# Moving the keys' adding transfers behind GpSimd's second long product, and one matrix product into the start, in a fused attention and feed-forward kernel

## The chip, the cores and the metric

The kernel runs on one core of one Trainium2 chip. The metric is the device time of one execution in microseconds; the median of several runs is compared. TensorE does matrix products, VectorE (DVE), ScalarE (ACT) and GpSimd (POOL) the elementwise work, and SyncE (SP) and GpSimd issue transfers.

## The reference

Attention over keys that are averaged over 4 x 4 places, for 4 batches of 12,288 queries with 128 channels and 768 keys, then a feed-forward layer of width 2048 with g = h - tanh(h):

```
kv_pool = kv.reshape(B, H // r, r, W // r, r, C).mean(axis=(2, 4))   # r = 4
k = v = kv_pool.reshape(B, -1, C) @ w_sr
s = (q @ k.T) / sqrt(C);  a = exp(s - s.max(-1));  a /= a.sum(-1) + 1e-09
x = a @ v
h = x @ w_in;  out = (h - tanh(h)) @ w_out
```

## The kernel before

**Groups and steps.** The queries go in 96 groups of 512, 24 for each batch. A group is 8 steps (UN) of the schedule. `attention` computes scores, exponentials and shares of a group some 20 steps ahead, `feed_forward` the 16 blocks of the hidden layer, in pairs, so 8 per group. The hidden function is a cubic around a centre, so every batch has its own scaled weights (`winr`, `Wr`), slopes (`At`, `Ah`) and centre (`cen`), which `keys` and `about_centre` prepare while the batch before it runs.

**Order.** No engine chooses at run time. Every operation is given to `Plan.op` with a due step, an engine, an assumed duration and the tiles it reads and writes. `Plan.run` plays this through once, with those durations, and the order that comes out is the order in which each engine's instructions are written. A tile named in an operation's reads orders the plan; on the chip an instruction waits only for what it really touches. Operations with `lane=True` keep the order of their due steps on their engine. `bank(.., "x", ..)` names one PSUM bank that is used by many in turn.

**GpSimd in a steady group.** In this order: `dr` (L832, the rounded part of the attention result), `z` = v + 1 (L903), [an adding transfer of the next batch's keys, L366, when there is one], `z` = z * v (L907, the first long product), the first adding transfer of the shares (`rs`, L797), `rp` = z * v (L907, the second long product), `dl` (L858), `ql` (L812), the second adding transfer of the shares (L797). `rp` feeds the last matmuls of `acc` in TensorE (L927), whose end lets ScalarE write the result `o` (L938).

**Keys of batches 2 to 4.** The 16 places are summed by transfers into one tile, `kvp`: one plain transfer from SP and 15 adding ones from GpSimd's queue, one per group, from `GATHER` groups ahead of the batch. Each waits for the one before it. Behind the last, VectorE sums the rows (L428) and takes the mean (L432).

**Keys of batch 1.** Twelve pieces of 64 keys are loaded at the start (L380), each with 16 values per key. VectorE sums eight of them (L394), GpSimd folds pieces 2, 5, 8 and 11 in four steps (L388). Ten matmuls (five of 512 columns, `warm`, L414) run on the summed pieces and their result is not used. Then come the mean (L433), `centre` (L440) and the first products with the centre (L536). The loads of the output weights and of q are ordered behind the sum of piece 6 (`HELD`).

**Norm of the input weights.** 16 matmuls `winT` x `winT` (32 instructions, fp32 takes two each; L333), a copy (L337) and one more product (L346) are due at step 16, in the steady groups.

Of the kernel before, what the change touches and what calls it, by code (L numbers as in the profile page):

```python
# [22 lines left out]
KB = 64  # L23
WN = 512
# [132 lines left out]
def attention_then_ffn(ctx: ExitStack, tc: tile.TileContext, q, kv_by_key, kv_by_place, w_sr, w_in,  # L157
                       w_out, out):
    nc = tc.nc
    V, A, PL, PE, SP = nc.vector, nc.scalar, nc.gpsimd, nc.tensor, nc.sync  # L160

    B, C, N = q.shape
    K, W = kv_by_key.shape[1], kv_by_key.shape[2]
    F = w_in.shape[1]
    KT, FT = K // P, F // P
    KH, UN, AN = K // 2, FT // 2, KT // 2
    NG = N // G
# [6 lines left out]
    dram = ctx.enter_context(tc.tile_pool(name="dram", bufs=1, space=DRAM))  # L174
    plan = Plan(tc)

    DIRECT, HELD = 2, 6
    BUFS = {"kc": 2, "kvp": 1, "kTr": 2, "vvr": 2, "Mn": 1, "Mh": 2, "A": 2, "Ah": 2, "Wg": 3, "Wr": 2,
            "winr": 2, "q": 4, "qr": 5, "ql": 2, "E": 2, "r2": 7, "rs": 3, "t": 2, "dl": 1, "df": 1, "dr": 2, "u": 3, "r": 4,
            "rp": 2, "v": 2, "z": 1, "o": 2, "row": 2, "col": 2, "At": 2, "hb": 2, "W2": 1,  # L180
# [2 lines left out]
    def sb(key, tag, shape, dt=F32, step=-1e6):  # L183
        n = BUFS[tag]
        plan.tile(key, tag, n, lambda: wk.tile(shape, dt, tag=tag, name=tag, bufs=n), step)

    def big(key, step):
        plan.tile(key, "big", 3, lambda: ps.tile([P, WIDE], F32, tag="big", name="big", bufs=3), step)

    def bank(key, tag, step):  # L190
        plan.tile(key, tag, 1, lambda: ps.tile([P, G], F32, tag=tag, name=tag, bufs=1), step)
# [6 lines left out]
    winT = const.tile([P, FT, C], F32, name="winT")  # L198
# [3 lines left out]
    ident = const.tile([P, P], F32, name="ident")  # L202
# [102 lines left out]
    def weights(step, load_step):  # L305
        NW = F // WN
        for n in range(NW):
            words_of(step + n, load_step + n / 8, n, "i")
        for j in range(2):
            turned = f"turned.{j}"  # L310
            big(turned, step + NW + j)
            for k in range(2):
                def turn(j=j, k=k, turned=turned):
                    for f in range(8 * j + 4 * k, 8 * j + 4 * k + 4):
                        PE.matmul(out=plan[turned][:, (f % 8) * P : (f % 8 + 1) * P],
                                  lhsT=win32[:, f * P : (f + 1) * P], rhs=ident,
                                  start=True, stop=True)

                plan.op(step + NW + j, "PE", 1.0, turn, (("win32", 2 * j + k), "ident"),
                        ((turned, k),), late=0.2)  # L320

            def copy(j=j, turned=turned):
                A.copy(out=winT[:, 8 * j : 8 * j + 8].rearrange("p t c -> p (t c)"), in_=plan[turned])

            plan.op(step + NW + j, "ACT", 1.03, copy, (turned,), (("winT", j),), late=0.1)
        s = 16.0
        bank("WW", "x", s)
        sb("WW32", "W2", [P, P])
        bank("W4", "x", s + 1)

        def product():
            for f in range(FT):
                PE.matmul(out=plan["WW"][:, 0:P], lhsT=winT[:, f], rhs=winT[:, f], start=(f == 0),  # L333
                          stop=(f == FT - 1))

        def copy_product():
            A.copy(out=plan["WW32"], in_=plan["WW"][:, 0:P])  # L337

        plan.op(s, "PE", 4.0, product, ("winT",), ("WW",), late=0.2)
        plan.op(s, "ACT", 0.3, copy_product, ("WW",), ("WW32",), late=0.1)  # L340
        norm(s + 1, "WW32", "W4", B)

    def norm(step, of, at, n):

        def square():
            PE.matmul(out=plan[at][:, 0:P], lhsT=plan[of], rhs=plan[of], start=True, stop=True)  # L346

        def rows():
            V.tensor_reduce(out=norms[:, n : n + 1], in_=plan[at][:, 0:P], op=ALU.add, axis=AX.X,
                            apply_absolute_value=True)  # L350

        plan.op(step, "PE", 0.25, square, (of,), (at,), late=0.2)
        plan.op(step, "DVE", 0.3, rows, (at,), (("norms", n),))

    def keys(b, s0):

        kvp, row, cen, kTr, vv32, vvr, Mn = (
            f"{x}.{b}" for x in ("kvp", "row", "cen", "kTr", "vv32", "vvr", "Mn"))
# [3 lines left out]
        NK = K // KB  # L362
        for w in range(W if b else 0):
            def gather(w=w):
                if w:
                    PL.dma_start(out=plan[kvp], in_=kv_by_place[b - 1, w], accum_op=ALU.add)  # L366
                else:
                    SP.dma_start(out=plan[kvp], in_=kv_by_place[b - 1, w])

            at = (b * NG - GATHER[b - 1] + max(w - 1, 0)) * UN + AT["more"][0] - 2 * UN  # L370
            plan.op(at - (0.01 if w else 4), *(("POOL", 0.87) if w else ("SP", 0.5)), gather, (), (kvp,),
                    late=3.0, dma=1.0, lane=w > 0)
        for j in range(0 if b else NK):
            gap = 0.1
            s, key = s0 - gap * (NK - j) - 2, f"kc.{b}.{j}"
            sb(key, ("E", "r", "rp", "kc", "r", "r")[j % 6], [P, KB, W])
            at = slice(j * KB, (j + 1) * KB)

            def load(at=at, key=key):
                SP.dma_start(out=plan[key], in_=kv_by_key[:, at, :])  # L380

            plan.op(s - 8, "SP", 0.5, load, (), (key,), late=2.0, dma=1.27)
            if j % 3 == 2:
                for k, w in enumerate((8, 4, 2, 1)):
                    def fold(key=key, w=w, at=at):
                        x = plan[key]
                        to = plan[kvp][:, at].unsqueeze(2) if w == 1 else x[:, :, 0:w]
                        PL.tensor_tensor(out=to, in0=x[:, :, 0:w], in1=x[:, :, w : 2 * w], op=ALU.add)  # L388

                    plan.op(s + k / 8, "POOL", 0.2 + KB * w * 0.0021, fold, (key,),  # L390
                            ((kvp, j),) if w == 1 else (key,))
            else:
                def pool(key=key, at=at):
                    V.tensor_reduce(out=plan[kvp][:, at], in_=plan[key], op=ALU.add, axis=AX.X)  # L394

                plan.op(s, "DVE", 1.2, pool, (key,), ((kvp, j), "held") if j == HELD else ((kvp, j),))
# [5 lines left out]
        sb(Mn, "Mn", [P, C])  # L402
        Mh = f"Mh.{b}"
        sb(Mh, "Mh", [P, 2, C], R32)
        apart_by = (1, 5.3, 8, 8)[b]
        s1, s2, s3, s4 = (s0 + n * apart_by for n in range(1, 5))
        s4 = s4 if b else 24.0
        for x, at in ((pc, s0), (pm, s3), (p4, s4)):
            bank(x, "x", at)
        if b == 0:  # L410
            big("warm", s0 - 3)
            for j in range(WN // KB - 1, NK):
                def warm(j=j):
                    PE.matmul(out=plan["warm"][:, 0:WN], lhsT=ident,  # L414
                              rhs=plan[kvp][:, (j + 1) * KB - WN : (j + 1) * KB], start=True,
                              stop=True)

                plan.op(s0 - 3, "PE", 1.2, warm, ["ident"] + [(kvp, i) for i in range(j + 1)],
                        ("warm",))
        big(pk, s1)  # L420
        big(pv, s2)

# [71 lines left out]
        for j in range(2):  # L494
            plan.op(s2 + j / 4, "PE", 0.7, partial(product_by_key, j), ("wsr", kvp), ((pv, j),),
                    late=0.2)
# [7 lines left out]
    def about_centre(b, s0):  # L504
# [12 lines left out]
        sb(Wr, "Wr", [P, FT, C], R32)  # L517
        FS, CS, AS, APART, SA, TA, WI, WS = EARLY if b < 2 else LATER
        first_at = [s0 + FS * n if b else s0 - 9.9 + n / 4 for n in range(4)]
# [86 lines left out]
        if b:  # L606
            plan.op(known, on, 2.2, first_order, (hb,), (hb, gg), late=MORE)
            plan.op(known + CS, on, 1.9, slopes_of, (hb,), (hb,))
# [62 lines left out]
        for n in range(NW):  # L671
# [27 lines left out]

            plan.op(slopes_at[n], "POOL", 1.1, by_first, (gg, "winT"), ((wg, 0),), late=MORE if b else 0.0)  # L700
            plan.op(slopes_at[n], "ACT", 0.2, beside, (gg,), ((wg, 1),), late=0.1)
# [26 lines left out]
    AT = dict(  # L728
        forth=[3.94, 1.06, 1.67, 5.41, 0.16, 6.02, 6.63, -0.46],
        first=[4.44, 1.51, 2.12, 5.84, 0.59, 6.45, 7.06, -0.02],  # L730
        then=[6.19, 2.26, 3.01, 6.54, 1.52, 7.28, 8.03, 0.77],
        back=[11.04, 6.93, 7.24, 7.85, 6.32, 8.76, 9.37, 5.71],
        scores=[-20.66, -21.57, -19.38], exps=[-20.16, -21.13, -18.94],
        beyond=[-19.46, -20.25, -18.25], values=[-3.75, -5.26, -4.35],
        more=[6.92, 9.07],
        copied=-18.59, added=[-15.50, -11.66],
# [122 lines left out]

        plan.op(s0 + AT["lower_left"], "POOL", 1.29, lower_left, (df, dr), (dl,), lane=True)  # L860

    EARLY = (2, 4.4, 5, 3.5, 8, 15, 22, 8)
    LATER = (4, 9, 9, 7, 16, 34, 31, 9)
    MORE = 2
    ON_POOL = (0,)

    def feed_forward(g, s0):
# [276 lines left out]
    LEAD = 20.0  # L1144
    start(-LEAD - 80)
    weights(-LEAD - 50, -LEAD - 60)
    plan.tile("held", "held", 1, lambda: None)
    GATHER = (24, 30, 30)
    KEYS, ABOUT = 104, 96
    KEYS1, ABOUT1 = 61, 60  # L1150
    SL = 6
# [76 lines left out]
```

## Time and profile before

| | |
|---|---|
| Time, median of 3 runs | 1312.98 us (1312.15 to 1314.66) |
| Profiled execution, its own time | 1312.51 us, span 1310.7 us |
| Busy share of the span | PE 97%, DVE 93%, ACT 91%, POOL 87% |
| Issue of an adding transfer of the keys | 45, median 875 ns |
| Weight product, L333 | 32 instructions, 3.7 us |

The profile is of one execution. Busy shares are means over stages with different limits, so the table says only that four engines are nearly full; which of them sets the end of a stretch is read from the stretch. A row of GpSimd can begin while the row before it has not ended, so starts and ends are compared, not durations alone.

### The profile page before, as it was taken

How to read it: one execution, taken by the hardware profiler on the slowest of the kernel's cores; microseconds unless marked ns; L12 is line 12 of the kernel's file. 1: busy time of each engine (PE TensorE's matmuls, PEld its weight loads, DVE VectorE, ACT ScalarE, POOL GpSimd, SP SyncE). 2: the span in 40 equal slices, each digit the busy share in tenths (PEclk: the TensorE clock that was granted, in tenths of full speed). 3: DMA queues.
4: the chain of work that ended last, by engine and by line, in shares of the span. 5: the costliest groups of instructions: out<-in, count | busy, mean ns of one | idle time of the engine just before them, and what ended most of it. 6: DMA issues, size and time to landing. Idle time of an engine off the chain costs nothing.

```text
span 1310.7 us, 17375 instructions
## 1 busy us (share of the span) xinstructions
PE 1267.8 (97%) x5520; PEld 888.8 (68%) x5520; DVE 1221.1 (93%) x1201; ACT 1196.2 (91%) x1423; POOL 1142.7 (87%) x969
## 2 busy tenths in 40 slices
PE   5899999999999999999999999999999999999997
PEld 3666666776666667767666666776766767667665
DVE  7789999898999998999999999899999999899996
ACT  4689999898999998999999999899999999899995
POOL 3578999899999997999999998899988888888896
PEclk9899999999999999999999999999999999999999
DMA  9165666545666654345666664344344444344431
GB/s 354 47 122 128 139 133 143 111 116 127 135 136 137 139 121 110 104 122 117 134 138 139 133 137 114 92 120 114 96 107 111 107 105 109 93 107 105 110 86 37
DMA packets 82708, 158.47 MB, mean 121 GB/s; under 512 B 9936, under 2 KB 12112, under 8 KB 82608
## 3 DMA queue, kind: packets, MB, share of 16 engines
q0 software_dynamic: 33552, 66.99, 31.4%
q1 hardware_dynamic: 49056, 90.29, 19.4%
q8 instruction: 45, 0.74, 0.2%
q14 instruction: 55, 0.45, 0.1%
HBM read 57.93 MB, written 25.39 MB: 64 GB/s over the span
## 4 chain that ended last, share of the span: by engine, by line
PE 42%; POOL 40%; ACT 8%; issue 5%; DVE 3%; DMA 2%; POOLq 0%; SPq 0%; ACTq 0%; DVEq 0%
PE acc L927 12%; PE big L889 11%; POOL rp L907 10%; POOL z L907 10%; POOL rs L797 5%; PE big L774 5%; PE x L818 4%; POOL z L903 4%; ACT E L778 4%; POOL dr L832 3%; POOL ql L812 3%; PE acc L878 2%; PE x L808 2%; ACT v L900 2%; ACT o L938 2%
## 5 line engine op out<-in xcount | busy, mean ns | idle before, releaser
L896 DVE SCALAR_TENSOR_TENSOR r<-big,u 128x1024 fp32r<-128x1024 f32 x672 | 778.4, 1217 | 24.9 <-ACT u L893 23.7
L893 ACT ACTIVATE u<-big 128x1024 f32<-128x1024 f32 x672 | 662.0, 1035 | 35.2 <-PE big L889 24.5
L889 PE MATMUL big<-dr,winr 128*128 128x512 f32 x1536 | 510.0, 413 | 1.6 <-DVE r L896 0.7
L927 PE MATMUL acc<-r,Wr 128*128 128x512 f32 x1344 | 426.1, 409 | 0.6 <-DVE r L896 0.6
L781 DVE SCALAR_TENSOR_TENSOR r<-E,big 128x1024 f16<-128x1024 f32 x288 | 350.2, 1217 | 41.1 <-ACT E L778 37.8
L889 PEld LDWEIGHTS big<-dr,winr 128*128 128x128 f32 x1536 | 276.8, 188 | 95.6 <-DVE r L781 23.5
L778 ACT ACTIVATE E<-big 128x1024 f32<-128x1024 f32 x288 | 296.1, 1029 | 16.4 <-PE big L774 6.0
L927 PEld LDWEIGHTS acc<-r,Wr 128*128 128x128 f32 x1344 | 251.7, 188 | 64.7 <-DVE r L896 1.5
L907 POOL TENSOR_TENSOR rp<-z,v 128x1024 fp32r<-128x1024 f32 x96 | 272.8, 2841 | 0.2
L907 POOL TENSOR_TENSOR z<-z,v 128x1024 f32<-128x1024 f32 x96 | 247.6, 2579 | 4.3
L797 POOL DMA_DIRECT2D rs<-r x188 | 222.0, 1181 | 5.9 <-DVE r L896 3.3
L774 PE MATMUL big<-qr,kTr 128*128 128x512 f32 x576 | 197.9, 425 | 4.4 <-ACT qr L759 1.6
L818 PE MATMUL x<-r,vvr 128*128 128x512 f16 x576 | 174.9, 386 | 0.0
L812 POOL TENSOR_TENSOR ql<-q,qr 128x512 fp32r<-128x512 f32 x96 | 163.3, 1701 | 5.2 <-ACT qr L759 5.2
L858 POOL TENSOR_TENSOR dl<-df,dr 128x512 fp32r<-128x512 f32 x96 | 163.7, 1706 | 0.0
L832 POOL TENSOR_SCALAR dr<-df 128x512 fp32r<-128x512 f32 x96 | 66.6, 694 | 108.5 <-DVE df L829 106.4
L774 PEld LDWEIGHTS big<-qr,kTr 128*128 128x128 f32 x576 | 105.0, 190 | 45.9 <-DVE r L781 15.0
L903 POOL TENSOR_SCALAR z<-v 128x1024 f32<-128x1024 f32 x96 | 107.8, 1123 | 0.0
L900 ACT COPY v<-big 128x1024 f32<-128x1024 f32 x96 | 97.8, 1018 | 1.1 <-PE big L889 1.0
L818 PEld LDWEIGHTS <-vvr 128*128 128x128 f16 x576 | 33.5, 98 | 79.4 <-issue 79.1
L938 ACT ACTIVATE o<-acc,At 128x512 f32<-128x512 f32 x96 | 65.7, 684 | 21.6 <-PE acc L927 21.4
L927 PE MATMUL acc<-rp,Wr 128*128 128x512 f32 x192 | 73.8, 466 | 10.8 <-POOL rp L907 7.7
(184 smaller groups left out, 1007.0 us busy)
## 6 DMA issues: line engine op xcount, KB each, us to landing
rs<-r POOLq DMA_DIRECT2D x188, 256.0 KB, 3.9
q<-in_q_dram SPq DMA_DIRECT2D x96, 256.0 KB
out_dram<-o SPq DMA_DIRECT2D x96, 256.0 KB
rs<-r SPq DMA_DIRECT2D x94, 256.0 KB
kvp<-in_kv_by_place_dram POOLq DMA_DIRECT2D x45, 384.0 KB, 5.0
r<-in_kv_by_key_dram SPq DMA_DIRECT2D x6, 512.0 KB
kc<-inverse SPq DMA_DIRECT2D x12, 256.0 KB
u<-in_moe_w_in_dram SPq DMA_DIRECT2D x3, 512.0 KB
```

The source lines that it names most:

```text
L774: PE.matmul(out=half(plan[s], h), lhsT=plan[kTr][:, n * P : (n + 1) * P], rhs=plan[qr], start=True, stop=True)
L778: A.activation(out=plan[e], in_=plan[s], func=AF.Exp)
L781: V.scalar_tensor_tensor(out=plan[r], in0=plan[e], scalar=-1.0, in1=plan[s], op0=ALU.add, op1=ALU.subtract)
L797: PL.dma_start(out=plan[rs], in_=plan[r2s[k]], accum_op=ALU.add)
L812: PL.tensor_tensor(out=plan[ql], in0=plan[qs], in1=plan[qr].bitcast(F32), op=ALU.subtract)
L818: PE.matmul(out=plan[num], lhsT=plan[vvr][:, n], rhs=half(plan[f"r2.{g}.{k}"], h), start=(start and h == 0), stop=(stop and h == 1))
L858: PL.tensor_tensor(out=plan[dl], in0=plan[df], in1=plan[dr].bitcast(F32), op=ALU.subtract)
L889: PE.matmul(out=half(plan[hp], h), lhsT=plan[winr][:, f * P : (f + 1) * P], rhs=plan[dr], start=True, stop=True)
L893: A.activation(out=plan[u], in_=plan[hp], func=AF.Square)
L896: V.scalar_tensor_tensor(out=plan[r], in0=plan[hp], scalar=1.0, in1=plan[u], op0=ALU.add, op1=ALU.mult)
L907: PL.tensor_tensor(out=plan[to], in0=plan[x], in1=plan[y], op=ALU.mult)
L927: PE.matmul(out=plan[acc], lhsT=plan[Wr][:, 2 * n + h], rhs=half(plan[r], h), start=(start and h == 0), stop=(stop and h == 1))
```

## The change

- The 45 adding transfers take their due step from `AT["more"][1]`, plus 0.01, in place of `AT["more"][0]`, minus 0.01: on GpSimd's queue they stand behind the second long product and not ahead of the first. The plain transfer on SP stays 4 steps ahead of the first one's step. `GATHER` goes from 30 to 29 for the third and fourth batch.
- The five `warm` matmuls are gone. The weight product, in two halves, its copy and its square go from step 16 to the start, ahead of `centre`; in the plan the halves wait for pieces 7 and 10 of the keys, which they do not touch.
- Piece 1 is summed by 16 matmuls with the identity on TensorE and copied by ScalarE, piece 11 by VectorE. Pieces 2, 5 and 8 stay on GpSimd. `HELD` is piece 9.
- Due steps of the preparation of batches 2 to 4 change: `apart_by` for batch 2, and EARLY, LATER and MORE.

```
-    DIRECT, HELD = 2, 6
+    DIRECT, HELD = 2, 9
+    BY_PE, BY_POOL = (1,), (2, 5, 8)
...
-        s = 16.0
+    def norm_of_weights(s):
...
-        def product():
-            for f in range(FT):
+        def product(h):
+            for f in range(h * FT // 2, (h + 1) * FT // 2):
                 PE.matmul(out=plan["WW"][:, 0:P], lhsT=winT[:, f], rhs=winT[:, f], start=(f == 0),
                           stop=(f == FT - 1))
...
-        plan.op(s, "PE", 4.0, product, ("winT",), ("WW",), late=0.2)
+        for h in range(2):
+            plan.op(s, "PE", 1.9, partial(product, h), (("winT", h), ("kvp.0", (7, 10)[h])), ("WW",), late=0.2)
...
-            at = (b * NG - GATHER[b - 1] + max(w - 1, 0)) * UN + AT["more"][0] - 2 * UN
-            plan.op(at - (0.01 if w else 4), *(("POOL", 0.87) if w else ("SP", 0.5)), gather, (), (kvp,),
+            at = (b * NG - GATHER[b - 1] + max(w - 1, 0)) * UN + AT["more"][1] - 2 * UN
+            plan.op(at + (0.01 if w else -4), *(("POOL", 0.87) if w else ("SP", 0.5)), gather, (), (kvp,),
                     late=3.0, dma=1.0, lane=w > 0)
...
-            if j % 3 == 2:
+            if j in BY_PE:
+                sums = f"sums.{j}"
+                bank(sums, "x", s)
+
+                def together(key=key, sums=sums):
+                    for w in range(W):
+                        PE.matmul(out=plan[sums][:, 0:KB], lhsT=ident, rhs=plan[key][:, :, w],
+                                  start=(w == 0), stop=(w == W - 1))
+
+                def keep(sums=sums, at=at):
+                    A.copy(out=plan[kvp][:, at], in_=plan[sums][:, 0:KB])
+
+                plan.op(s, "PE", 2.4, together, ("ident", key), (sums,), late=0.2)
+                plan.op(s, "ACT", 0.25, keep, (sums,), ((kvp, j),), late=0.1)
+            elif j in BY_POOL:
...
-        apart_by = (1, 5.3, 8, 8)[b]
+        apart_by = (1, 6, 8, 8)[b]
...
-            big("warm", s0 - 3)
-            for j in range(WN // KB - 1, NK):
-                def warm(j=j):
-                    PE.matmul(out=plan["warm"][:, 0:WN], lhsT=ident,
-                              rhs=plan[kvp][:, (j + 1) * KB - WN : (j + 1) * KB], start=True,
-                              stop=True)
-
-                plan.op(s0 - 3, "PE", 1.2, warm, ["ident"] + [(kvp, i) for i in range(j + 1)],
-                        ("warm",))
+            norm_of_weights(s0 - 0.6)
...
-    EARLY = (2, 4.4, 5, 3.5, 8, 15, 22, 8)
-    LATER = (4, 9, 9, 7, 16, 34, 31, 9)
-    MORE = 2
+    EARLY = (2.5, 4.4, 4, 6, 8, 18, 24, 8)
+    LATER = (4, 6, 9, 7, 18, 30, 31, 7)
+    MORE = 2.5
...
-    GATHER = (24, 30, 30)
+    GATHER = (24, 29, 29)
```

## Rows read from the trace of the kernel before

**Rows 1.** The page's chain that ended last, share of the span by engine.

```profile
PE 42%; POOL 40%; ACT 8%; issue 5%; DVE 3%; DMA 2%; POOLq 0%; SPq 0%; ACTq 0%; DVEq 0%
```

**Rows 2.** Stretches between results, L938 alone: length, ScalarE busy (xresults), clock, DMA.

```profile
82.20:98.70 16.50, 0.69 (x1) 1.00 0.55 114
98.70:236.90 138.20, 7.55 (x11) 1.00 0.63 136
282.20:352.10 69.90, 3.43 (x5) 1.00 0.60 130
352.10:477.80 125.70, 6.88 (x10) 1.00 0.63 137
626.90:790.20 163.30, 8.95 (x13) 1.00 0.64 137
950.80:1097.50 146.70, 8.16 (x12) 1.00 0.44 108
```

**Rows 3.** Timeline of GpSimd, a group with an adding transfer: start, length in us.

```profile
406.69 1.05 POOL L903 TENSOR_SCALAR z<-v 128x1024 f32<-128x1024 f32 x1
...
408.31 2.71 POOL L907 TENSOR_TENSOR z<-z,v 128x1024 f32<-128x1024 f32 x1
```

**Rows 4.** Timeline of GpSimd, a late group without an adding transfer.

```profile
998.29 1.53 POOL L858 TENSOR_TENSOR dl<-df,dr 128x512 fp32r<-128x512 f32 x1
...
1000.77 1.13 POOL L797 DMA_DIRECT2D rs<-r  x1
1003.40 0.62 POOL L832 TENSOR_SCALAR dr<-df 128x512 fp32r<-128x512 f32 x1 [1.49 <-DVE df L829]
1003.99 1.05 POOL L903 TENSOR_SCALAR z<-v 128x1024 f32<-128x1024 f32 x1
1005.13 2.42 POOL L907 TENSOR_TENSOR z<-z,v 128x1024 f32<-128x1024 f32 x1
```

**Rows 5.** Chain of waits between 380 and 420 us: start, length, what.

```profile
401.78 0.74 PE acc L927 x2
...
402.55 0.69 ACT o L938
```

**Rows 6.** Timeline of TensorE, the same late group.

```profile
1002.51 0.40 PE L878 MATMUL acc<-dl,Ah 128*128 128x512 f32 x1
...
1007.47 0.60 PE L802 MATMUL x<-rs,share 128*128 128x512 f16 x2
```

**Rows 7.** Timeline of TensorE, the weight product.

```profile
88.10 3.73 PE L333 MATMUL x<-winT 128*128 128x128 f32 x32
```

**Rows 8.** The long groups: PE, PEld, DVE, ACT, POOL busy (xinstructions); then L685 alone.

```profile
282.20:352.10 69.90, 66.15 (x298) 46.72 (x297) 63.32 (x61) 61.64 (x75) 69.90 (x58) 1.00 0.60 130
...
282.20:352.10 69.90, 4.29 (x32) 4.11 (x32) 1.00 0.60 130
```

**Rows 9.** Line 366: ns min/median/max, first and last start; landing in us.

```profile
L366 POOL DMA_DIRECT2D kvp<-in_kv_by_place_dram x45: 862/875/1946, 45.5 to 782.9; - x45
...
DMA to landing us min/median/max: 4.6/5.0/6.3
```

**Rows 10.** Timeline of VectorE, the mean of the fourth batch's keys.

```profile
804.96 0.17 DVE L432 TENSOR_REDUCE row<-row 128x1 f32<-128x24 f32 x1
```

**Rows 11.** Timeline of the start: TensorE, SyncE's queue and VectorE.

```profile
11.37 3.78 PE L315 MATMUL big<-ident,win 128*128 128x128 f32 x16 [0.53 <-DVE win L288]
...
16.13 3.18 SPq L380 DMA_DIRECT2D r<-in_kv_by_key_dram  x2
...
23.51 6.66 PE L414 MATMUL big<-kvp,ident 128*128 128x512 f32 x10 [4.67 <-DVE kvp L394]
...
28.25 0.15 DVE L433 TENSOR_SCALAR row<-row 128x1 f32<-128x1 f32 x1
...
30.53 3.73 PE L536 MATMUL acc<-col,win 128*128 128x1 f32 x32 [0.25 <-DVE col L443]
```

**Rows 12.** A stretch of the start: PE, PEld, DVE, ACT, POOL busy, PEclk, DMA, GB/s.

```profile
48.00:51.00 3.00, 1.78 (x3) 1.01 (x4) 3.00 (x4) 1.26 (x4) 0.62 (x1) 0.55 0.55 104
```

## The prediction

> **What bounds the kernel now.** I read the chain of waits first. It belongs to TensorE and GpSimd in almost equal parts [rows 1], so the question is where each of them rules. The second view is the stretches between two `result` activations (L938, one for each group of 512 queries) [rows 2]. Twelve late groups take 146.7 us, 12.225 each. The early groups, in which one adding transfer of the next batch's keys is issued per group, take 138.2 / 11 = 12.56, 125.7 / 10 = 12.57 and 163.3 / 13 = 12.56. Two stretches stand out: one group of 16.50 us, and five groups of 69.9 us.
>
> Why a group with a transfer is 0.34 us longer is seen on GpSimd's timeline. With it [rows 3], `z<-v` ends at 407.74 and the first long product at 411.02, 3.28 us later. Without it [rows 4], the same two ends are 1005.04 and 1007.55, 2.51 us apart. So the transfer's issue moves the products by 3.28 - 2.51 = 0.77 us. In the chain [rows 5] the end of the second product `rp` lets TensorE start the last two matmuls of `acc` at 401.78; ScalarE's `o` follows at 402.55, and behind it in their orders the exponentials, VectorE's `df` and GpSimd's `dr`, which leads to the next product. That loop includes the issue, and it is the loop that sets 12.56. Without a transfer the loop has room, and TensorE's own work sets 12.225.
>
> **The gathers' new place: 11.5 us.** Nothing is added or removed, 45 issues move from before the first product to behind the second one: past L907 `z`, the first adding transfer of the shares (L797) and L907 `rp`. `rp` then comes 0.77 us earlier for its group, as in the late groups. What is now behind the issue on GpSimd's queue is `dl`, `ql`, the second `rs` transfer and `dr`. Without an issue there GpSimd stands idle 1.49 us before `dr`, ended by VectorE's `df` [rows 4]. The issue takes 0.77 of that and 0.72 stays, so `dr` isn't later. `dl` ends at 998.29 + 1.53 = 999.82 and its matmul starts at 1002.51, 2.69 us of cover; the `rs` transfer is issued at 1000.77 and read at 1007.47, 6.7 us later [rows 4, 6]. Both covers are over 0.77. If the cover before `dr` is gone, each microsecond of price over 1.49 comes back in each group. So the period should be TensorE's 12.225. From [rows 2]: 138.2 - 11 x 12.225 = 3.72, 125.7 - 10 x 12.225 = 3.45, 163.3 - 13 x 12.225 = 4.37; the sum is 11.5 us. From below the gain is nothing (the new place has no room), from above it is these 11.5, since TensorE then has no gap left.
>
> **The product of the input weights: 4.3 us.** Its 32 matmuls take 3.73 us in the middle of the steady groups [rows 7], in the one group of 16.50 us [rows 2]. 16.50 - 12.56 = 3.9 us, the product and its square and waits. TensorE has no gap to hide it. That group holds a gather as well, 0.34. Both leave: 4.3 (16.50 - 12.225).
>
> **The stretch of five long groups: 1.5 us.** 69.9 - 5 x 12.225 = 8.8 us are over the bare groups [rows 2]. The 32 slope matmuls (L685) are TensorE's own part, 4.3 us [rows 8], which stays. About 4.5 are left, with one transfer in each group. GpSimd is busy for all its 69.90 us [rows 8] (its scalings for the next batch), so moving an issue inside gives nothing; but the third batch's transfers begin one group and two steps later (29 for 30), so one or two of five leave. The new due times of the scalings (EARLY, LATER, MORE) spread their work; the trace has no row for the order that results. Bounds: +2 us (they bunch elsewhere) and -4.5 (all of it goes). I take two issues, 2 x 0.77 = 1.5, as GpSimd is the engine that fills it.
>
> **The last gather of the third and fourth batch: nothing.** It moves by one group and 2.15 of 8 steps, 1.27 x 12.225 = 15.5 us. For the fourth batch it starts at 782.9, so at 798.4, and lands 5.0 later, at 803.4 [rows 9]. The mean of the keys is taken at 804.96 on VectorE [rows 10]; that leaves 1.5 us for the six row sums ahead of it, about what they need. If they come 1 us late, VectorE waits, with the cubes (L896) behind, and TensorE for them: at most 1 us for each of two batches.
>
> **The start: nothing, between -1.5 and +6.3.** Before, the ten idle matmuls hold TensorE for 6.66 us from 23.51, to 30.17, though the centred mean is ready at 28.25 + 0.15 = 28.40 [rows 11]; that costs some 1.6 us, and they go. Piece 11 goes from GpSimd's four folds to one VectorE sum, which can take about a microsecond more off the mean. Piece 1 goes to TensorE: 16 fp32 matmuls, 32 instructions, which stand between the second and third of the four turns of the weights if the order follows the landings. The rows nearest to them are L536, 32 in 3.73 us (0.117 each), and L315, 16 in 3.78 (0.236 each) [rows 11]: 3.7 to 7.6 us. From about 13.2 (the eighth of the sixteen L315) it ends at 16.9 or 20.8; the load that needs its buffer left at 16.13 before [rows 11] and SP's queue (two keys' pieces, output weights, q) stands behind it. Then come two turns and the product, 3.7 or 7.6 us, and `centre` waits for the copy of the product too, as both use the one bank `x`: ready between 28.5 and 32.5. The best is 1.5 us before today's 30.0; the worst is 2.5 behind, plus 3.8 if L536 itself ran at the slow rate, (0.236 - 0.117) x 32. I take 0, since the gain is certain in kind and the loss depends on the clock.
>
> On the clock: with TensorE busy 1.78 of 3 us, the stretch at 48 shows a granted clock of 0.55, close to its 1.2 GHz level [rows 12], and the L315 above ran at twice the later time per instruction. The Trainium skill, page "TensorE: Matmul & The Clock Gate", section "Part 1: The HAM clock gate", says that activity releases a throttle and a pause brings it back, so dropping matmuls that only keep the array busy is the wrong way round. No run here shows it for this place. By it the sum would be 1299.0, 3.8 us more for L536; by the L536 row as it stands, 1295.2.
>
> **The sum.** 11.5 + 4.3 + 1.5 = 17.3 us. The profiled execution took 1312.51 us for a span of 1310.7, and 1312.51 - 17.3 = 1295.2; it lies 0.5 below the median of the runs, 1312.98. I say 1295.
>
> **Rivals.** (1) The new place has no room: GpSimd's `dl`, `ql` and second transfer become the late ones, and groups with a transfer stay at 12.56. For it: its idle time before `dr` is only 1.49 and transfers share the queue; against it: covers of 0.72, 1.9 and over 5 us stay. 1295.2 + 11.5 = 1306.7.
> (2) The start turns cold: product and L536 run at the slow rate, 3.8 us, up to 6.3 with a late `centre`. For it: the L315 row and TensorE's pause between product and mean; against it: the product itself is 32 instructions of work shortly before. 1299.0 to 1301.5.
> (3) The new due times bunch GpSimd's scalings or the last gathers land late: a loss of 2 for the gain of 1.5, and 2 more, 1300.7. For it: GpSimd has no gap in the long stretch [rows 8]; against it: two transfers less fall there.
> (4) Slower: in the new place an issue costs more than it did. At a price p the period is 12.225 + (p - 1.49); over 34 groups the 17.3 us are eaten up at p = 1.49 + 17.3 / 34 = 2.0 us, and every microsecond beyond costs 34. For it: the longest issue shown took 1.946 [rows 9]; against it: the median is 0.875. At 2.2 it gives 1319.
>
> **How the numbers follow.** The forecast has 0.60, rival 1 0.12, rival 2 0.16, rival 3 0.07, rival 4 0.05. The forecast's own range is 1291 to 1299. 1289 takes in the lower bounds together (4.5 instead of 1.5 in the long groups and 1.5 at the start, 1290.7) and 1.5 for what separates one execution from another; 1304 takes in rivals 2 and 3, also with a part of both. Rivals 1 and 4 are left out, 0.17. A measurement of this kernel tells about 0.2%, 2.6 us, from no change. Faster by more: all but rival 4 and the worst of the others together, 0.92; within: 0.04; slower: 0.04.
>
> **What would show it.** Right: the groups with a transfer take 12.2 to 12.3 us, with TensorE without gaps and GpSimd idle about 0.7 us before `dr`; the group of 16.5 is gone; the five long groups take 67 to 69. Wrong: a wait of TensorE for `dl` or `rs`, `dr` starting right behind an `rs` transfer, or slow matmuls of L536 after the mean. What would make the number wrong is above all a longer stretch of GpSimd at a change of batch, where no row shows the new order.

## The result and the profile after

The changed kernel takes 1296.76 us in the median of four runs (1296.01 to 1300.68), the kernel before 1313.68 us beside it (1312.15 to 1314.66): a ratio of 0.9878, 95% interval 0.9855 to 0.9901. The profiled execution took 1296.01 us for a span of 1294.3. Lines of the code have moved: L938 is now L946, L907 L915, L858 L866, L797 L805, L366 L368, L536 L544.

The chain that ended last, by engine, answers to [rows 1]:

```profile
PE 67%; POOL 22%; issue 5%; ACT 2%; DVE 2%; DMA 1%; SPq 0%; POOLq 0%; DVEq 0%; ACTq 0%
```

GpSimd's share has gone from 40% to 22%. The stretches between results answer to [rows 2]: length, ScalarE busy (xresults), clock, DMA.

```profile
84.10:96.44 12.34, 0.68 (x1) 1.00 0.67 139
96.44:231.37 134.93, 7.49 (x11) 1.00 0.65 140
277.58:344.14 66.56, 3.41 (x5) 1.00 0.56 129
344.14:467.33 123.19, 6.80 (x10) 1.00 0.64 139
616.06:775.44 159.38, 8.85 (x13) 1.00 0.65 140
935.82:1082.50 146.68, 8.16 (x12) 1.00 0.44 108
```

A group with a transfer now takes 134.93 / 11 = 12.27, 123.19 / 10 = 12.32 and 159.38 / 13 = 12.26 us in the mean, for 12.56 before. The late groups are what they were, 12.22; most groups with a transfer take that too, and the means are higher by a few groups (the first of each stretch: 12.48, 13.19 and 12.66). The group of 16.50 us takes 12.34, the five long groups 66.56 for 69.90. GpSimd's timeline in a group with a transfer:

```profile
392.54 1.17 POOL L368 DMA_DIRECT2D kvp<-in_kv_by_place_dram  x1
393.15 1.88 POOL L866 TENSOR_TENSOR dl<-df,dr 128x512 fp32r<-128x512 f32 x1
...
395.63 1.49 POOL L805 DMA_DIRECT2D rs<-r  x1
397.67 0.62 POOL L840 TENSOR_SCALAR dr<-df 128x512 fp32r<-128x512 f32 x1 [0.55 <-DVE df L837]
...
399.39 2.41 POOL L915 TENSOR_TENSOR z<-z,v 128x1024 f32<-128x1024 f32 x1
...
405.37 1.91 POOL L866 TENSOR_TENSOR dl<-df,dr 128x512 fp32r<-128x512 f32 x1
```

GpSimd is idle 0.55 us ahead of `dr`, where a group without a transfer had 1.49 [rows 4]: the issue costs 1.49 - 0.55 = 0.94 us in its new place, and the cover holds it. TensorE reads the `dl` that ends at 405.37 + 1.91 = 407.28 at 409.01, 1.73 us later:

```profile
409.01 0.40 PE L886 MATMUL acc<-dl,Ah 128*128 128x512 f32 x1
```

The row of the transfers themselves answers to [rows 9]; the median row is longer than before's 875 ns, though a row's length isn't what it delays:

```profile
L368 POOL DMA_DIRECT2D kvp<-in_kv_by_place_dram x45: 1027/1172/1202, 63.3 to 786.2; - x45
...
DMA to landing us min/median/max: 4.7/5.2/6.2
```

The start answers to [rows 11]. TensorE first, then SyncE's queue, then VectorE:

```profile
13.61 6.93 PE L391 MATMUL x<-r,ident 128*128 128x64 f32 x32
20.34 3.71 PE L316 MATMUL big<-ident,win 128*128 128x128 f32 x16
23.85 3.92 PE L334 MATMUL x<-winT 128*128 128x128 f32 x32
30.20 0.35 PE L448 MATMUL x<-row,wsr 128*128 128x1 f32 x2 [2.42 <-ACT o L283]
30.80 3.37 PE L544 MATMUL acc<-col,win 128*128 128x1 f32 x16 [0.25 <-DVE col L451]
...
34.59 3.41 PE L544 MATMUL acc<-col,win 128*128 128x1 f32 x16
37.87 2.91 PE L455 MATMUL big<-kvp,wsr 128*128 128x384 f32 x4
```

```profile
20.57 0.33 SPq L382 DMA_DIRECT2D r<-in_kv_by_key_dram  x1
```

```profile
24.81 1.22 DVE L410 TENSOR_REDUCE kvp<-r 128x64 f32<-128x1024 f32 x1 [2.39 <-DMA r<-in_kv_by_key_dram]
...
29.94 0.15 DVE L441 TENSOR_SCALAR row<-row 128x1 f32<-128x1 f32 x1
```

TensorE's summing of piece 1 takes 6.93 us. The load that needs that piece's buffer leaves at 20.57 (before: 16.13), VectorE waits 2.39 us for it, and the mean is ready at 30.09 (before: 28.40). TensorE, out of work at 27.77, pauses 2.42 us; then the 32 matmul instructions of the centre's first products take 3.37 + 3.41 us where [rows 11] had 3.73. The granted clock there, TensorE busy, clock, DMA share, GB/s:

```profile
30.00:33.00 3.00, 2.56 (x14) 0.68 1.08 397
33.00:36.00 3.00, 3.00 (x16) 0.50 0.51 188
36.00:39.00 3.00, 3.00 (x12) 0.50 0.32 90
39.00:42.00 3.00, 3.00 (x13) 0.62 0.00 0
```

The same four stretches before had 1.00, 0.77, 0.66 and 1.00. Of the last gathers, the one for the third batch comes just late, by 0.24 us on VectorE (its answer to [rows 10], one step earlier in the row sums):

```profile
483.38 1.25 DVE L436 TENSOR_REDUCE row<-kvp 128x4 f32<-128x128 f32 x6 [0.24 <-DMA kvp<-in_kv_by_place_dram]
```

Where the time went, up to the last result, as the difference of the two profiled executions over each stretch of groups, counted from 0; the last column is a second profiled execution of the changed kernel (e11 below) against the same one of before. The prediction worked out 10 and 13 groups where the table has 11 (21 to 31) and 14 (42 to 55):

| stretch | working of the prediction | after | after, again |
|---|---|---|---|
| up to the first result | 0 | +1.90 | +1.36 |
| group 1 (it had the weight product) | -4.3 | -4.18 | -4.29 |
| groups 2 to 12, a transfer each | -3.72 | -3.25 | -3.21 |
| groups 13 to 20, change of batch | -1.5 | -2.48 | -0.80 |
| groups 21 to 31, a transfer each | -3.45 | -2.59 | -2.59 |
| groups 32 to 41, change of batch | 0 | -0.27 | -0.14 |
| groups 42 to 55, a transfer each | -4.37 | -4.05 | -4.02 |
| groups 56 to 80 | 0 | 0.00 | +0.13 |
| group 81 | 0 | -1.48 | -1.45 |
| groups 82 to 95 | 0 | -0.08 | -0.06 |
| sum | -17.3 | -16.48 | -15.07 |

### The profile page after: what moved, and what is told of

The parts are those of the page before. It is cut to its first block, busy times and chain, and to the rows that moved or that the text cites. A ratio compares the mean times of both kernels' runs of the same rounds, so it can differ in the third digit from the quotient of the medians.

```text
span 1294.3 us, 17417 instructions
## 1 busy us (share of the span) xinstructions
PE 1261.0 (97%) x5542; PEld 893.3 (69%) x5542; DVE 1219.8 (94%) x1201; ACT 1192.6 (92%) x1424; POOL 1144.6 (88%) x965
## 4 chain that ended last, share of the span: by engine, by line
PE 67%; POOL 22%; issue 5%; ACT 2%; DVE 2%; DMA 1%; SPq 0%; POOLq 0%; DVEq 0%; ACTq 0%
PE big L897 20%; PE acc L935 19%; PE big L782 8%; PE x L826 7%; POOL rp L915 5%; POOL z L915 4%; PE x L816 4%; PE acc L886 4%; POOL rs L805 3%; PE x L810 2%; POOL ql L820 2%; POOL z L911 2%; POOL dr L840 2%; POOL dl L866 1%; DVE r L904 1%
## 5 line engine op out<-in xcount | busy, mean ns | idle before, releaser
L915 POOL TENSOR_TENSOR rp<-z,v 128x1024 fp32r<-128x1024 f32 x96 | 257.2, 2679 | 0.2
L915 POOL TENSOR_TENSOR z<-z,v 128x1024 f32<-128x1024 f32 x96 | 231.8, 2415 | 7.9
L805 POOL DMA_DIRECT2D rs<-r x188 | 204.3, 1087 | 3.9 <-DVE r L904 1.9
L782 PE MATMUL big<-qr,kTr 128*128 128x512 f32 x576 | 193.6, 417 | 2.3 <-DVE r L789 0.8
L866 POOL TENSOR_TENSOR dl<-df,dr 128x512 fp32r<-128x512 f32 x96 | 162.6, 1694 | 0.0
L840 POOL TENSOR_SCALAR dr<-df 128x512 fp32r<-128x512 f32 x96 | 70.4, 734 | 83.7 <-DVE df L837 77.5
L782 PEld LDWEIGHTS big<-qr,kTr 128*128 128x128 f32 x576 | 101.5, 188 | 49.9 <-DVE r L789 27.6
L911 POOL TENSOR_SCALAR z<-v 128x1024 f32<-128x1024 f32 x96 | 111.6, 1162 | 0.0
L946 ACT ACTIVATE o<-acc,At 128x512 f32<-128x512 f32 x96 | 65.4, 681 | 11.4 <-PE acc L935 10.6
```

The costliest lines, as they stand in the source:

```text
L782: PE.matmul(out=half(plan[s], h), lhsT=plan[kTr][:, n * P : (n + 1) * P], rhs=plan[qr], start=True, stop=True)
L805: PL.dma_start(out=plan[rs], in_=plan[r2s[k]], accum_op=ALU.add)
L866: PL.tensor_tensor(out=plan[dl], in0=plan[df], in1=plan[dr].bitcast(F32), op=ALU.subtract)
L915: PL.tensor_tensor(out=plan[to], in0=plan[x], in1=plan[y], op=ALU.mult)
```

## The experiments

All but e11 change only what their diffs show; every kernel computes the whole reference. Each was timed beside the kernel before: its median is 1314.16 us beside e1 to e4, 1312.89 beside e5 to e8, 1312.43 beside e9 to e11, so ratios are what to compare.

**e1: the gathers' place alone, in the kernel before.**

```
-            at = (... + max(w - 1, 0)) * UN + AT["more"][0] - 2 * UN
-            plan.op(at - (0.01 if w else 4), ...
+            at = (... + max(w - 1, 0)) * UN + AT["more"][1] - 2 * UN
+            plan.op(at + (0.01 if w else -4), ...
```

> The kernel before with the one edit that its gathers stand behind the second long product; GATHER, the warm matmuls, the weight product and all other due steps as before. Theory (the gather fits into GpSimd's pause before dr): the groups with a gather go from 12.56 to 12.22 us, which over 34 to 36 groups is 10 to 12 us, so 1302 to 1304 against 1313.7, with the 16.5 us group still there less 0.3. Rival (the gain came from the other edits, the new due steps among them): groups with a gather stay above 12.45 and the time stays above 1309.

1299.40 us, ratio 0.9892 (0.9873 to 0.9912): better than expected, 14.8 us for the place alone. The groups with transfers give 3.12 (groups 2 to 12), 3.56 (21 to 31) and 4.09 (42 to 55), near the working. But 2.77 us come before the first result, which I hadn't counted. [Rows 9] show where: before, the first issue stands at 45.5, in the start, ahead of GpSimd's scalings for the first batch's weights. In e1 the first issue comes at 59.08, TensorE's first slope matmuls (L685), which read those scalings, start at 46.88 in place of 51.45, and the half clock at 48 to 54 (0.55 in [rows 12]) is gone. Three of the 45 issues stand ahead of the first result, and all three have moved. TensorE to GpSimd busy, clock, DMA, GB/s of e1:

```profile
48.00:51.00 3.00, 1.52 (x5) 0.71 (x6) 3.00 (x3) 1.64 (x6) 0.74 (x1) 1.00 0.00 0
51.00:54.00 3.00, 3.00 (x19) 2.31 (x18) 3.00 (x6) 1.79 (x3) 1.09 (x2) 1.00 0.00 1
```

**e2: the changed kernel with the gathers back ahead of the first product.**

```
-            at = (... + max(w - 1, 0)) * UN + AT["more"][1] - 2 * UN
-            plan.op(at + (0.01 if w else -4), ...
+            at = (... + max(w - 1, 0)) * UN + AT["more"][0] - 2 * UN
+            plan.op(at - (0.01 if w else 4), ...
```

> The changed kernel with its gathers put back ahead of the first long product, GATHER at 24, 29, 29 as in the change. Theory: the groups with a gather are 12.56 again, and the time is that of the changed kernel plus 10 to 12, 1307 to 1309. Rival (place and other edits need each other, or other edits made the gain): less than 5 us above the changed kernel's 1296.8.

1308.39 us, ratio 0.9961 (0.9946 to 0.9976), as expected. Against the changed kernel the place is worth 10.9 us by the ratios (11.6 by the medians); in the profiles 2.1 us of it come before the first result. Groups 13 to 20 are 2.28 us shorter than before here, with the transfers in their old place, and 0.12 longer in e1, with the new place alone: what they gain comes from the due times and the later begin of the transfers.

**e3: two of the five `warm` matmuls back (four instructions), between the product and the centre.**

```
+            big("warm", s0 - 3)
+            for j in range(NK - 2, NK):
+                def warm(j=j):
...
+                plan.op(s0 - 3, "PE", 1.2, warm, ["ident"] + [(kvp, i) for i in range(j + 1)], ("warm",))
```

> The changed kernel with two of the five idle matmuls of 512 columns (those on pieces 3 to 10 and 4 to 11) put back between the weight product and the centre. Theory (the start is late because TensorE pauses 2.4 us before the mean and then runs the 32 first products at half rate): the 32 instructions take 3.7 us in place of 6.8, the first winr is 2 to 3 us earlier and the first result comes 1 to 3 us earlier than at 84.2, so 1294 to 1296. Rival (the start is late only because the held load of piece 10 makes the mean late): the first products are no faster, and the first result is at 84 or later.

1295.92 us, ratio 0.9867 (0.9847 to 0.9886), as expected. TensorE pauses 0.53 us ahead of the centre in place of 2.42, and the first products run at full rate, 1.95 + 1.89 us:

```profile
27.17 2.04 PE L431 MATMUL big<-kvp,ident 128*128 128x512 f32 x4
29.74 0.35 PE L457 MATMUL x<-row,wsr 128*128 128x1 f32 x2 [0.53 <-ACT o L283]
30.34 1.95 PE L553 MATMUL acc<-col,win 128*128 128x1 f32 x16 [0.25 <-DVE col L460]
...
32.45 1.89 PE L553 MATMUL acc<-col,win 128*128 128x1 f32 x16
```

The next work starts at 34.21, where before had 34.13 and the changed kernel 37.87; the first result is 3.7 us earlier than in the changed kernel's profile. The medians differ by less than their intervals.

**e4: TensorE sums piece 3 in place of piece 1.**

```
-    BY_PE, BY_POOL = (1,), (2, 5, 8)
+    BY_PE, BY_POOL = (3,), (2, 5, 8)
```

> The changed kernel with piece 3 and not piece 1 summed on TensorE. No later load needs the buffer of piece 3. Theory of the held load: piece 10 is issued at about 16 in place of 20.6 us, the stretch 18 to 24 us shows transfers without a gap, the mean is ready 1 to 2 us earlier than at 30.1, and the first result up to 2 us earlier than 84.2. Theory of the clock: the first products start earlier but still run at half rate if the pause before them stays, 6.8 us for 32, so the first result gains no more than the mean does. Rival: no difference, as the weight product ends later than the mean.

1294.35 us, ratio 0.9858 (0.9837 to 0.9879). No load is held (two leave from 16.03), and the mean's last step starts at 28.02. The first half of the centre's products takes 2.09 us, the second 3.41 again, and the next work starts at 34.72. So the held load and the low clock are two costs of the start. The first result comes 3.5 us earlier than in the changed kernel's profile, more than the mean does (1.9 us), against the expectation.

```profile
28.32 0.35 PE L448 MATMUL x<-row,wsr 128*128 128x1 f32 x2 [1.08 <-DVE row L441]
28.93 2.09 PE L544 MATMUL acc<-col,win 128*128 128x1 f32 x16 [0.25 <-DVE col L451]
...
31.45 3.41 PE L544 MATMUL acc<-col,win 128*128 128x1 f32 x16
```

**e5: each adding transfer as two of half the columns, in the new place.**

```
-                    PL.dma_start(out=plan[kvp], in_=kv_by_place[b - 1, w], accum_op=ALU.add)
+                    for h in range(2):
+                        at = slice(h * K // 2, (h + 1) * K // 2)
+                        PL.dma_start(out=plan[kvp][:, at], in_=kv_by_place[b - 1, w][:, at], accum_op=ALU.add)
```

> The changed kernel with every adding transfer of keys on GpSimd's queue issued as two, each of half the columns, one right behind the other, in the same new place. The theory of the cover: in the changed kernel GpSimd still waits 0.55 us ahead of dr in a group with a gather, so a second issue of the 0.95 us that the first one costs there uses that up and leaves 0.40 us, a period of 12.6 us again in the 34 groups with a gather: 34 x 0.40 = 13.6, a median near 1310 us (1306 to 1314), with the idle time ahead of dr gone. A rival, by which the price goes with the bytes, or by which what counted was only that no issue stands ahead of the first product: both halves together cost what one did, or lie under cover, the period stays at 12.2 and the time at 1296 to 1298 us.

1317.14 us, ratio 1.0027 (1.0018 to 1.0036): slower than the kernel before. GpSimd's timeline, the pair of issues and what is behind it:

```profile
400.89 2.08 POOL L370 DMA_DIRECT2D kvp<-in_kv_by_place_dram  x2
402.03 2.24 POOL L868 TENSOR_TENSOR dl<-df,dr 128x512 fp32r<-128x512 f32 x1
...
405.61 1.42 POOL L842 TENSOR_SCALAR dr<-df 128x512 fp32r<-128x512 f32 x1
...
408.12 2.41 POOL L917 TENSOR_TENSOR z<-z,v 128x1024 f32<-128x1024 f32 x1
```

The idle time ahead of `dr` is gone. From the issue to the next first product it is 408.12 - 400.89 = 7.23 us; with one issue it was 399.39 - 392.54 = 6.85, of which 0.55 idle: the second issue, of half the bytes, costs 7.23 - 6.30 = 0.93 as well. The steady groups:

```profile
96.72:234.71 137.99, 7.54 (x11) 1.00 0.64 137
364.17:490.02 125.85, 6.88 (x10) 1.00 0.64 136
```

137.99 / 11 = 12.54 and 125.85 / 10 = 12.585, 0.3 to 0.4 over 12.22, as 0.93 - 0.55 = 0.38 says. The miss of 3 us against the upper end expected (1314) lies for the most part in groups at a change of batch that have no cover: 18 to 21 and 42 take 0.86 to 0.92 us more each, nearly the whole second issue. Groups 32 and 56 hold no issue; there VectorE waits for the last transfers to land (0.28 + 0.61 and 0.79 us). Group 32 is 2.2 us longer, but part of that is a granted clock of 0.59 at 497 to 500: in e10, with one issue, the same group is 2.1 us longer at a clock of 0.50 (485 to 488).

**e6: piece 3 and the two idle matmuls together** (the diffs of e3 and e4).

> The changed kernel with TensorE summing piece 3 instead of piece 1 and with the last two of the idle matmuls put back between the product of the weights and the centre. If the late load of piece 10 (1.5 to 1.7 us of the mean) and the half clock behind the pause ahead of the centre (some 2 us) are two costs of the start, they add: the first result some 1.3 us earlier than with either alone, a median of 1292 to 1294 us. If they are one cost, seen twice, then no earlier than with piece 3 alone: 1294 to 1296 us.

1296.98 us, ratio 0.9880 (0.9864 to 0.9897), over both ranges expected; the two don't add. The idle matmuls wait for the last pieces, and the second half of the product, ordered behind them, ran at 26.64; the centre waited 1.02 us for the copy of it. The products ran at or near full rate all the same:

```profile
30.24 1.95 PE L553 MATMUL acc<-col,win 128*128 128x1 f32 x16 [0.25 <-DVE col L460]
...
32.35 2.25 PE L553 MATMUL acc<-col,win 128*128 128x1 f32 x16
```

The next work starts at 34.47, close to e3's 34.21 and e4's 34.72. Yet the first result is 2.9 us later than e3's and 1.1 later than before's, though the gather is out of the start. The difference arises behind 34.47, with more time at the low clock: 0.50 at 36 to 39 and 0.72 at 63 to 66, where e3 had 0.75 and 1.00. Why the clock fell at 63 here and not there stays open.

**e7: the product in the place of the idle matmuls alone, in the kernel before.**

```
-        s = 16.0
+    def norm_of_weights(s):
...
-            big("warm", s0 - 3)
-            for j in range(WN // KB - 1, NK):
...
+            norm_of_weights(s0 - 0.6)
```

> The kernel before with one part of the change: the product of the input weights in two halves in the place of the idle matmuls. Pieces 1 to 11 are summed, their loads held, and the gathers and due times set as before. The theory: group 1 loses its 4.2 us, and the start gives most or all of it back, because the pause ahead of the centre leaves TensorE at half clock in the batched work behind it: the first result 1.5 to 4 us later than before, a median of 1310 to 1314 us. The rival, by which what makes the changed kernel's start late is TensorE's summing of piece 1 and the load held by it alone: first result as before, 1309.5 us, and a granted clock at 33 to 39 us no lower than before's 0.77 and 0.66.

1311.40 us, ratio 0.9988 (0.9978 to 0.9998), as expected. Group 1 is 3.96 us shorter and the first result 3.52 us later: the move by itself is nearly a wash. TensorE's start:

```profile
17.68 3.74 PE L334 MATMUL x<-winT 128*128 128x128 f32 x32
28.08 0.56 PE L448 MATMUL x<-row,wsr 128*128 128x1 f32 x2 [6.66 <-issue]
28.89 3.58 PE L544 MATMUL acc<-col,win 128*128 128x1 f32 x16 [0.25 <-DVE col L451]
```

No piece is summed on TensorE here and no load held by one, so a pause, here of 6.66 us, is enough for slow products.

**e8: the due times back.**

```
-    EARLY = (2.5, 4.4, 4, 6, 8, 18, 24, 8); LATER = (4, 6, 9, 7, 18, 30, 31, 7); MORE = 2.5
+    EARLY = (2, 4.4, 5, 3.5, 8, 15, 22, 8); LATER = (4, 9, 9, 7, 16, 34, 31, 9); MORE = 2
...
-        apart_by = (1, 6, 8, 8)[b]
+        apart_by = (1, 5.3, 8, 8)[b]
...
-    GATHER = (24, 29, 29)
+    GATHER = (24, 30, 30)
```

> The changed kernel with the due times of the planner as before: the two lists that order the thresholds' work, the extra of later groups, the spacing of the second batch's steps, and the groups at which the gathers of batches 2 and 3 begin. The theory: the edits of due times are what takes 2.2 us out of the groups 13 to 21 that hold the first batch of new keys, and little elsewhere: a median near 1299 us (1298 to 1301). The rival: those groups are shorter from the gathers' place alone, or by chance: 1296 to 1297.5 us.

1299.24 us, ratio 0.9890 (0.9873 to 0.9906), as expected: by the ratios 1.6 us over the changed kernel, with intervals that overlap. In the profile groups 13 to 20 are 1.72 us longer than before, not 2.48 shorter. 1.6 of these 4.2 us are a low clock in group 13 (16.18 us; 14.58 in the changed kernel's first profile), which e11 shows too; 2.6 are the due times, with one transfer more among them: here the third batch's begin in group 16, in the changed kernel in group 17. Group 21 gives 0.97 of them back (12.22 us here, 13.19 in the changed kernel), so that 1.6 us are left, as the ratios have it.

**e9: piece 3, and the idle matmuls behind the product** (e6 with the matmuls due at `s0 - 0.5`).

> The changed kernel with TensorE summing piece 3 instead of piece 1, and the last two pairs of idle matmuls due 0.1 us behind the product of the weights, not ahead of it: in e6 they were due earlier, and the second half of the product waited behind them and held the centre up by 1.0 us. The theory of two costs: the load of piece 10 is not held and TensorE has work until shortly before the centre, so the first result comes 1 to 2 us earlier than with either edit alone, a median of 1292 to 1294.5 us. If the first result comes no earlier than with piece 3 alone (1.6 us ahead of the kernel before), the two do not add, and the median is 1294 to 1297 us.

1295.83 us, ratio 0.9872 (0.9856 to 0.9888), in the range of "do not add". TensorE's order is the one wanted, but behind the idle matmuls it pauses 0.56 us for the mean and 1.15 for VectorE's copy of the centre; the products then take 3.37 + 3.41 us, and the first result is 0.9 us later than before's.

**e10: the pieces and all ten idle matmuls as before, the product in TensorE's gaps ahead of them.**

```
-    DIRECT, HELD = 2, 9
-    BY_PE, BY_POOL = (1,), (2, 5, 8)
+    DIRECT, HELD = 2, 6
+    BY_PE, BY_POOL = (), (2, 5, 8, 11)
...
-            plan.op(s, "PE", 1.9, partial(product, h), (("winT", h), ("kvp.0", (7, 10)[h])), ("WW",), late=0.2)
+            plan.op(s, "PE", 1.9, partial(product, h), (("winT", h),), ("WW",), late=0.2)
...
-            norm_of_weights(s0 - 0.6)
+            norm_of_weights(s0 - 3.5)
+            big("warm", s0 - 3)
+            for j in range(WN // KB - 1, NK):
...
```

> The changed kernel with the first key pieces summed, loaded and held as before, all ten idle matmuls back, and the product of the weights in TensorE's idle time around the third and fourth turn of the weights (before: 1.62 and 4.67 us idle there). The theory: all of the start's loss (3.7 us at 47 us) comes from the summing of piece 1 and from the idle matmuls left out; with both undone the mean is ready at 28.4 us, the batched work starts at 34.1 us as before, the first result comes 2 to 3 us earlier than before (the gather that no longer stands in the start's way), and the median is 1292 to 1294.5 us. The rival: the product itself, in front of the idle matmuls or of the copy of the weights, delays the start, or half clock comes again at another place: 1295 to 1298 us.

1297.92 us, ratio 0.9893 (0.9878 to 0.9907): the rival. TensorE, then its clock in the last column but two:

```profile
23.38 3.67 PE L431 MATMUL big<-kvp,ident 128*128 128x512 f32 x8 [0.41 <-DVE kvp L410]
27.62 1.13 PE L431 MATMUL big<-kvp,ident 128*128 128x512 f32 x2 [0.57 <-POOL kvp L404]
28.58 0.28 PE L457 MATMUL x<-row,wsr 128*128 128x1 f32 x2
29.93 6.27 PE L553 MATMUL acc<-col,win 128*128 128x1 f32 x32 [1.07 <-DVE col L460]
```

```profile
30.00:33.00 3.00, 3.00 (x18) 0.62 0.61 231
```

The ten idle matmuls took 6.66 us before [rows 11], up to the centre; behind the product they take 3.67 + 1.13 at a granted clock of 1.00 (24 to 30), end 1.4 us earlier, and TensorE pauses 0.57 and 1.07 us. (In e1, whose start is before's, they take 6.96 us, at 0.50 from 24 to 27 and 0.82 from 27 to 30.) Then the 32 products run at 6.27 us. That the idle matmuls were late was what kept TensorE busy until its next work.

**e11: the changed kernel once more.**

> The changed kernel once more, on the same chip and beside the same runs of the kernel before as the two others. For the differences of its stretches: those that the change makes come again (group 1 shorter by 4.2 us, some 0.33 us for each group with a gather, first result 1 to 3 us later than before); a difference that comes and goes with the granted clock (1.5 us in group 81, and part of the start's) may not. A median of 1296 to 1298 us.

1296.76 us, ratio 0.9877 (0.9860 to 0.9893), as expected. The table above has its stretches. What differs between the two profiles of one kernel is group 13, 16.16 us in place of 14.58, over a lower clock behind the same wait of 0.72 us (TensorE busy, clock, DMA, GB/s; e11 first, then the first profile):

```profile
238.00:244.00 6.00, 5.96 (x23) 0.72 0.26 46
```

```profile
238.00:244.00 6.00, 5.36 (x27) 1.00 0.28 54
```

Group 81 is 1.45 us shorter here again. It is so in e7 too, which has the place and the due times of before, and not in e1. Before's profile had a clock of 0.50 at 1127 to 1130, behind a pause of TensorE of 2.78 us; the changed kernel has that pause too, 2.83 us, and 1.00 behind it (1111 to 1114). So these 1.5 us are not put down to the change.

## Why the prediction was right, by its steps

The forecast, 1295, is 1.8 us under the median, and the faster sign, the range and the main mechanism held. Two terms were mis-sized and one step failed, in part against each other. Of the signs named ahead, those for right came or came close (0.55 us idle ahead of `dr` for 0.7, long groups of 66.56 us for 67 to 69); of those for wrong two came as well, the slow matmuls after the mean and, in group 21, a wait of TensorE for `dl` and `rp` (0.18 and 0.39 us).

- **The gathers' place, 11.5 us.** Right in mechanism and nearly in size: the three stretches give 9.8 to 9.9 us in the two profiles. The price was 0.94 us in the new place, not 0.77, and the idle time left 0.55, not 0.72; most groups take the 12.2 us that were forecast, the first of each stretch 0.25 to 0.97 more. The 0.97, in group 21, come with the due times and the later begin of the transfers: with those of before the group takes 12.22 (e1, e8), and the place alone gives 10.8 us in the three stretches (e1). What failed is the count: the step took 34 groups, but three transfers stand ahead of the first result as well, and moving them gave 2.8 us there (e1) or 2.1 (e2).
- **The cover rule and rival 4.** Its formula, 12.225 + (p - 1.49), was tried at p = 0.94 + 0.93 = 1.87 (e5): 12.605 by the formula, 12.54 to 12.585 measured. Rival 4 set the point at which the gain is lost at 2.0 us; e5 lost it at 1.87, for the most part since groups at the changes of batch have no cover at all and pay the whole issue; some of its loss is low clock.
- **The weight product, 4.3 us.** 4.18 and 4.29 measured, and 3.96 alone (e7).
- **The five long groups, 1.5 us.** 3.34 (69.90 to 66.56); groups 13 to 15 and 21 give back 1.5, so the term fits only as a net, 1.8. The cause named was two issues fewer; it is one. By e5 an issue there costs 0.9 us, and e8, which puts it and the due times back together, loses 1.6 us in groups 14 to 21. So the due times have a part; the two were not tried apart.
- **The last gathers, nothing.** One wait of 0.24 us.
- **The start, nothing.** This step failed: rival 2 came true for the first products with the centre. It took piece 1 to be summed in 3.7 to 7.6 us, and 6.93 it was; the load behind it left 4.4 us later, as the step feared. It then took the loss as open; what the runs show is 27.77 to 30.20 without work for TensorE, a granted clock of 0.68 and 0.50, and 6.78 us for products priced at 3.73, 3.05 more. At 37.87 for 34.13 the start is 3.74 us behind. That this is so near the 3.8 of rival 2 is in part chance: 0.27 are a later centre and 0.42 the square of the product (L348), which now stands between the two halves; the slow rate was 3.41 / 16 = 0.213 us and not 0.236; and the weight product, which rival 2 had slow as well, took 3.92. The Trainium skill, page "TensorE: Matmul & The Clock Gate", section "Part 1: The HAM clock gate", on which the prediction drew beside rival 2, agrees with e7 in direction: without the idle matmuls the first half of the products takes 3.58 us. That more work ahead is no cure when a pause follows is what e10 shows. At the first result only 1.90 and 1.36 us are left of the loss, because the gathers moved in the start pay 2.1 to 2.8.

So the forecast's number stands on errors that cancel: a start that lost some 3.5 to 4.7 us and gathers in it that gave 2 to 3; and in the profiles on the 1.5 us of group 81, which is luck as far as the runs show. A version of the start that is faster isn't shown. The profiles of e3 and e4 have the first result 1.8 and 1.6 us earlier than before's and group 1 as short as the changed kernel's, but each is the profile of the fastest of four runs; by the ratios e3, e4 and e9 are at 0.9867, 0.9858 and 0.9872, and their intervals all hold the changed kernel's 0.9878.

## What to carry to other kernels

An issue on an in-order queue costs by where it stands: look for the instruction on that queue that waits longest for another engine, and put the issue ahead of that wait and behind what others wait for; its idle time is the budget, and what exceeds it returns in every round (e5). Count all rounds, those of the start too. And before work that looks idle is removed, look at what it leaves: a pause ahead of a batch of matmuls may cost more than the work did.

## What the runs showed of the hardware

- An adding transfer on GpSimd's queue costs that engine by the issue and not by the bytes: 0.94 us for one of 384 KB, 0.94 + 0.93 for two of half as much (e5).
- The same 16 matmul instructions take 1.95 us at a granted clock of 1.00 (e3) and 3.41 at 0.50 (after), the levels of 2.4 and 1.2 GHz. Behind a pause of 0.53 us (e3) or 1.02 us (e6) they began at 1.00 and took 1.95; behind 2.42 us (after), or 0.57 and 1.07 in a row (e10), the clock fell, and behind 1.08 us it fell in their midst (e4: 2.09 us, then 3.41). The last pause alone doesn't decide it.
- One pause isn't one answer: behind the same wait of 0.72 us, in the same kernel, the clock stayed at 1.00 in one execution and was 0.72 over the next 6 us in the other, 1.6 us of time. A difference of that size between two single profiles is no evidence for a change until a second profile has it too.
